# Remainder rows in one load per input, an earlier release of loads, and a scaled identity made by ScalarE

## The chip, the cores and the metric

One of the cores of one Trainium2 chip runs the whole program. The metric is device time in microseconds of that core, from one launch to its end; the kernel before took 313.18 us (median of 3 runs). The five engines of the core have queues of their own: PE (TensorE), DVE (VectorE), ACT (ScalarE), POOL (GpSimd) and SP (SyncE). POOL issues all loads here, SP all stores.

## The reference: what is computed

Four batches of q, k and v come as float32 arrays of 6336 rows by 256 channels. Attention works across channels, then a gated feed-forward layer follows, row by row:

```python
qn = q / (norm(q, axis=1) + 1e-06);  kn = k / (norm(k, axis=1) + 1e-06)
s = kn.transpose(0, 2, 1) @ qn / tau            # 256 x 256 per batch
a = softmax(s, axis=-1)
x = (v @ a).reshape(25344, 256)
H = maximum(x @ w_h, 0);  T = sigmoid(x @ w_t + b_t)
out = T * H + (1 - T) * x
```

## The kernel before, in words

**Tiles.** A tile is 128 rows of one input by 256 channels. The 6336 rows of a batch are 49 full tiles and 64 rows over, the remainder. A load casts float32 to 16-bit float on the way; it brings 4 to 17 tiles, and the remainder of each batch comes by a small load of its own (lines 109 to 125): qr and kr into tiles of their own, that of v into the last slot of the batch's third v load. Loads are numbered through: five of q and five of k a batch (q0 to q19, k0 to k19, a ring of six buffers each), three of v a batch (v0 to v11, a ring of four).

**Phase 1** (`p1_tile`) runs over the 50 tiles of a batch and sums on PE the product S of k and q (line 185) and, in G, the products of k and of q with themselves (lines 188 and 191), whose diagonals are the squared norms.

**The chain** (`chain`, ten steps) turns S and G of a batch into the matrices `mr` of phase 2. Its steps: the diagonals on DVE (`junk`, line 209), the root by a power on POOL (`nrm`, line 216), the reciprocal on DVE (`inv`, line 222), the identity scaled by `inv` and 1/tau (`dcat`, line 225, two instructions on DVE), a PE product with a matrix of ones that spreads this row of factors over all partitions (`cq`, line 233), logits on DVE, exponentials on ACT (`ar`, with a table load before and one behind), the softmax scale on ACT, a transpose and two products with the weights on PE.

**Phase 2** takes 25 steps a batch, 100 in all, each for a pair of tiles of v. In step t (line 523) PE computes the gate sums z into one of two banks that hold the bias already (`zbank`), transposes the pair of step t + 3 (`vtps`, line 340), then computes h and x; all three are line 363. ACT takes the sigmoid (`tt`, line 393), copies the transposed pair for even t (`vts`, line 355; DVE does it for odd t; the last pair of a batch, with 64 rows in its second tile, is copied in two pieces, line 353) and refills the bank with the bias (line 397). DVE forms `th` and `ux` (lines 405 and 410), POOL subtracts them into the output tile (`o`, line 416), and SP stores each four steps (line 388). `vtps` has one buffer; h, x, `cq` and other chain products share three; `th` and `ux` have five each.

**The order of the work** is written out by hand. The first batch's phase 1 runs alone, then its chain, then the 100 steps; in between the steps PE takes tiles of the next batch's phase 1, by the table KNOTS (all 150 are done at step 64). The chains of batches 1, 2 and 3 begin at steps 19, 44 and 64, and their steps are spread over the following ones by STEPS. A chain step stands ahead of ("pre"), behind ("post") or behind the PE part ("pe") of a step's own work, on every engine on which it issues.

**The release of loads** is planned when the program is built. `want` (line 431) lists the loads by the step that needs them; after each step `next_loads` (line 462) puts up to two of them into POOL's queue, if their ring buffer is free by then and if, in a small model of the DMA queue (0.315 us a tile, stores counted in), the load that stands eight places back has landed. In the running kernel POOL stands at a load until the one eight places back has landed.

Of the kernel before, what the change touches and what calls it, by code (L numbers as in the profile page):

```python
# [9 lines left out]
AluOp = mybir.AluOpType  # L10
Act = mybir.ActivationFunctionType
# [8 lines left out]
def kernel(  # L20
# [73 lines left out]

    q_t, k_t, qr_t, kr_t, v_t = {}, {}, {}, {}, {}

# [16 lines left out]
    def load_kr(b):  # L113
        kr_t[b] = stream_pool.tile([P, C], f16, tag="k_rem", bufs=2, name=f"kr{b}")
        nc.gpsimd.dma_start(out=kr_t[b][0:REM, :], in_=k[b][NF:N, :])

    def load_v(m):
        b, g = VALL[m]
        s0, ns = VG[b][g]
        v_t[m] = stream_pool.tile([P, 18, C], f16, tag="v_in", bufs=VRING, name=f"v{m}")  # L120
        nc.gpsimd.dma_start(out=v_t[m][:, 0:ns, :], in_=rows(v[b])[:, s0 : s0 + ns, :])

    def load_vr(b):
        g = len(VG[b]) - 1
        nc.gpsimd.dma_start(out=v_t[VFIRST[b] + g][0:REM, VG[b][g][1], :], in_=v[b][NF:N, :])

# [10 lines left out]
    ones32 = const_pool.tile([P, P], f32, tag="ones32")  # L137
    nc.vector.memset(ones32, 1.0)
    half = const_pool.tile([P, 4], f32, tag="half")
    nc.vector.memset(half, 0.5)  # L140
# [18 lines left out]
    load_k(NQG)  # L159
    load_v(0)  # L160

    def hx_tile(name):
# [6 lines left out]
    def p1_tile(b, j):  # L169
# [4 lines left out]
        if j == NS:  # L174
            kk, qq, nr = kr_t[b], qr_t[b], REM
# [24 lines left out]
    def chain(b):  # L200
# [19 lines left out]
        def invs():  # L220
            inv = work_pool.tile([P, 4], f32, tag="inv", name=f"inv{b}")
            nc.vector.reciprocal(out=inv, in_=st["nrm"])
            dcat = work_pool.tile([P, 2, P], f32, tag="dcat", bufs=1, name=f"dcat{b}")
            for c in range(2):
                nc.vector.tensor_scalar(
                    out=dcat[:, c, :], in0=ident0, scalar1=inv[:, 2 + c : 3 + c],
                    scalar2=inv_tau, op0=AluOp.mult, op1=AluOp.mult,
                )
            st.update(inv=inv, dcat=dcat)

        def pe_cq():
            cq = hx_tile(f"cq{b}")
            nc.tensor.matmul(cq[:, 0, :], ones32, st["dcat"][:, :, :], start=True, stop=True)
            st["cq"] = cq
# [86 lines left out]

    vT_t = {}
    o_t = {}
    NSLOT = B * NPAIR

    def v_of(b, s):
        g = max(i for i in range(len(VG[b])) if VG[b][i][0] <= s)
        return v_t[VFIRST[b] + g], s - VG[b][g][0]

# [3 lines left out]
    def transpose(t):  # L333
        b, i = divmod(t, NPAIR)
        vt, s = v_of(b, 2 * i)
        ps = psum_pool.tile([P, 2, 2, P], f32, tag="vT", name=f"vtps{t}")
        nr = nrows(i)
        for u in range(2):
            for c in range(2):
                nc.tensor.matmul(  # L340
                    ps[:, u, c, 0 : nr[u]], vt[0 : nr[u], s + u, bass.ts(c, P)],
                    ident[0 : nr[u], 0 : nr[u]],
                    start=(u == 0 and c == 0), stop=(u == 1 and c == 1),
                )
        return ps

    def vt_copy(t, ps):
        i = t % NPAIR
        sb = work_pool.tile([P, 2, 2, P], f16, tag="vTs", bufs=LOOK + 2, name=f"vts{t}")
        cp = nc.vector.tensor_copy if t % 2 else nc.scalar.copy  # L350
        if i == NPAIR - 1:
            for u, r in enumerate(nrows(i)):
                cp(out=sb[:, u, :, 0:r], in_=ps[:, u, :, 0:r])
        else:
            cp(out=sb, in_=ps)  # L355
        vT_t[t] = sb
# [75 lines left out]
    for n in range(NQG + 1, B * NQG):  # L432
# [4 lines left out]
        want.append((at, len(want), load_k, n, dep, QG[b][g][1]))  # L437
    for b in range(1, B):
        at = p1_slot((b - 1) * (NS + 1) + NS)
        want.append((at - 1, len(want), load_qr, b, None, 0.5))  # L440
        want.append((at - 1, len(want), load_kr, b, None, 0.5))
    for m in range(1, len(VALL)):
# [3 lines left out]
        want.append((at, len(want), load_v, m, dep, VG[b][g][1]))  # L446
        if g == len(VG[b]) - 1:
            want.append((at, len(want), load_vr, b, None, 0.5))
    want.sort()
# [3 lines left out]
    LANES = 8  # L453
    TILE_US = 0.315
    landing = [0.0] * LANES
# [134 lines left out]
```

## Time and profile before

| | |
|---|---|
| median of 3 runs (lowest to highest) | 313.18 us (312.12 to 313.43) |
| the profiled execution | 313.83 us, its span 312.1 us |
| PE busy in the span | 267.4 us (86%) |
| DVE, ACT, POOL busy | 172.6, 162.8, 170.7 us |
| DMA moved | 65.58 MB, mean 210 GB/s |
| HBM read, written | 78.38 MB, 25.95 MB |
| granted TensorE clock, mean | 0.954 |

Rows of the profile name the engine, the line of the kernel, the operation and the tiles (written <- read). In a row of idle time, "<-" names what ended the wait. Times in rows of the timeline are from the start of the span; the span leaves out 1.76 us of the profiled execution's own time.

### The profile page before, as it was taken

The numbers are of one execution on the slowest core, as the hardware profiler recorded it, in microseconds if no ns is written. First come the engines' busy times: TensorE is split into PE (matmuls) and PEld (weight loads), VectorE is DVE, ScalarE is ACT, GpSimd is POOL, SyncE is SP. The second block draws the span as 40 slices with busy tenths as digits, with TensorE's granted clock in tenths as the row PEclk, the third lists the DMA queues.
The fourth block names the chain that finished last, engine by engine and source line by source line (L and its number), as shares of the span: only waits on it lengthen the run. The fifth ranks groups of instructions, "written<-read, shape, count | busy, mean of one in ns | idle before, by whom it ended". The sixth has DMA issues, their size and how long they took to land.

```text
span 312.1 us, 6905 instructions
## 1 busy us (share of the span) xinstructions
PE 267.4 (86%) x2844; PEld 233.2 (75%) x2844; DVE 172.6 (55%) x321; ACT 162.8 (52%) x298; POOL 170.7 (55%) x184
## 2 busy tenths in 40 slices
PE   0498977999999899999999429999999868999990
PEld 0397854999999687999997318798998645999960
DVE  0000023775555746666668503555557947999990
ACT  1000055654455586565567613455556677898860
POOL 6112330865555755665667502755557644788881
PEclk9999967999999999999999957999999979999996
DMA  6999999999989999999968596999999951435434
GB/s 119 213 215 214 211 209 219 215 253 285 232 222 211 246 263 235 264 266 250 307 110 222 152 209 108 244 236 247 243 269 260 202 214 41 162 135 221 186 137 160
DMA packets 13377, 65.58 MB, mean 210 GB/s; under 512 B 1569, under 2 KB 3618, under 8 KB 8738
## 3 DMA queue, kind: packets, MB, share of 16 engines
q0 software_dynamic: 8992, 39.19, 64.5%
q1 hardware_dynamic: 4354, 25.96, 20.7%
q8 instruction: 22, 0.36, 0.4%
q14 instruction: 9, 0.07, 0.1%
HBM read 78.38 MB, written 25.95 MB: 334 GB/s over the span
## 4 chain that ended last, share of the span: by engine, by line
PE 62%; DMA 17%; DVE 6%; POOL 5%; ACT 4%; issue 3%; POOLq 0%; DVEq 0%
PE h L363 11%; PE zbank L363 11%; PE x L363 11%; PE S L185 10%; DMA k<-in_k_dram 9%; DMA v<-in_v_dram 8%; PE vtps L340 6%; PE G L191 5%; PE G L188 5%; POOL o L416 2%; DVE ux L410 2%; DVE th L405 2%; DVE junk L209 1%; POOL k L107 1%; PE ah L286 1%
## 5 line engine op out<-in xcount | busy, mean ns | idle before, releaser
L416 POOL TENSOR_TENSOR o<-th,ux 128x512 f32<-128x512 f32 x96 | 124.2, 1295 | 104.4 <-DVE ux L410 81.3
L363 PEld LDWEIGHTS <-vts 128*128 128x128 f16 x1200 | 111.1, 99 | 17.3 <-issue 5.0
L185 PE MATMUL S<-q,k 128*128 128x256 f16 x392 | 90.2, 284 | 13.7 <-DMA k<-in_k_dram 13.6
L393 ACT ACTIVATE tt<-zbank 128x512 f32<-128x512 f32 x100 | 59.7, 597 | 79.3 <-PE zbank L363 78.7
L405 DVE SCALAR_TENSOR_TENSOR th<-h,tt 128x512 f32<-128x512 f32 (+1 forms) x104 | 68.8, 665 | 56.7 <-PE h L363 40.8
L188 PE MATMUL G<-k 128*128 128x128 f16 x392 | 78.8, 226 | 0.0
L410 DVE SCALAR_TENSOR_TENSOR ux<-tt,x 128x512 f32<-128x512 f32 (+1 forms) x104 | 67.8, 655 | 0.8 <-PE x L363 0.7
L363 PE MATMUL x<-mr,vts 128*128 128x256 f16 (+1 forms) x400 | 61.9, 277 | 0.9 <-DVE th L405 0.9
L363 PE MATMUL h<-mr,vts 128*128 128x256 f16 (+1 forms) x400 | 61.9, 277 | 0.0
L363 PE MATMUL zbank<-mr,vts 128*128 128x256 f16 (+1 forms) x400 | 61.6, 276 | 0.0
L397 ACT COPY zbank<-btb 128x512 f32<-128x512 f32 x98 | 58.7, 599 | 1.6
L191 PE MATMUL G<-q 128*128 128x128 f16 x392 | 55.8, 226 | 0.0
L185 PEld LDWEIGHTS <-k 128*128 128x128 f16 x392 | 39.9, 102 | 18.0 <-DMA k<-in_k_dram 14.0
L340 PE MATMUL vtps<-ident,v 128*128 128x128 f16 (+1 forms) x400 | 40.0, 223 | 14.0 <-DMA v<-in_v_dram 10.0
L355 DVE CAST vts<-vtps 128x512 f16<-128x512 f32 x48 | 33.0, 687 | 25.8 <-PE vtps L340 25.8
L340 PEld LDWEIGHTS <-v 128*128 128x128 f16 (+1 forms) x400 | 30.9, 100 | 18.7 <-DMA v<-in_v_dram 10.5
L188 PEld LDWEIGHTS <-k 128*128 128x128 f16 x392 | 39.9, 102 | 1.2 <-issue 0.3
L191 PEld LDWEIGHTS <-q 128*128 128x128 f16 x392 | 31.6, 102 | 2.9
L355 ACT CAST vts<-vtps 128x512 f16<-128x512 f32 x48 | 27.9, 580 | 9.9 <-PE vtps L340 9.8
L209 DVE SCALAR_TENSOR_TENSOR junk<-G,ident 128x128 f32<-128x128 f32 x16 | 3.7, 287 | 36.5 <-PE G L191 36.5
L488 ACT COPY btb<-btp 128x256 f32<-128x256 f32 x2 | 0.6, 375 | 37.5 <-PE btp L485 37.5
L101 POOL DMA_DIRECT2D q<-in_q_dram x20 | 11.3, 567 | 6.6 <-DMA q<-in_q_dram 4.5
(55 smaller groups left out, 102.8 us busy)
## 6 DMA issues: line engine op xcount, KB each, us to landing
out_dram<-o SPq DMA_DIRECT2D x24, 1024.0 KB, 7.7
q<-in_q_dram POOLq DMA_DIRECT2D x12, 768.0 KB, 18.2
k<-in_k_dram POOLq DMA_DIRECT2D x12, 768.0 KB, 18.2
v<-in_v_dram POOLq DMA_DIRECT2D x8, 1024.0 KB, 9.8
v<-in_v_dram POOLq DMA_DIRECT2D x4, 1088.0 KB, 18.0
q<-in_q_dram POOLq DMA_DIRECT2D x4, 576.0 KB, 8.5
k<-in_k_dram POOLq DMA_DIRECT2D x4, 576.0 KB, 12.0
q<-in_q_dram POOLq DMA_DIRECT2D x4, 256.0 KB, 9.7
```

Of the source, the lines that this page charges most:

```text
L101: nc.gpsimd.dma_start(out=q_t[n][:, 0:ns, :], in_=rows(q[b])[:, s0 : s0 + ns, :])
L185: nc.tensor.matmul(S[:, c, :], kc, qq[0:nr, :], start=first and c == 0, stop=last and c == 1)
L188: nc.tensor.matmul(G[:, c, :], kc, kc, start=first and c == 0, stop=False)
L191: nc.tensor.matmul(G[:, 2 + c, :], qc, qc, start=False, stop=last and c == 1)
L340: nc.tensor.matmul(ps[:, u, c, 0 : nr[u]], vt[0 : nr[u], s + u, bass.ts(c, P)], ident[0 : nr[u], 0 : nr[u]], start=(u == 0 and c == 0), st ...
L355: cp(out=sb, in_=ps)
L363: nc.tensor.matmul(dst[0:r, u, :], sb[:, u, kt, 0:r], mr[:, kt, off : off + C], start=(not seeded and kt == 0 and (u == 0 or i == NPAIR - 1)),
L393: nc.scalar.activation(out=tt, in_=z, func=Act.Sigmoid)
L397: nc.scalar.copy(out=z, in_=btb)
L405: nc.vector.scalar_tensor_tensor(out=th[pr, us, :], in0=h[pr, us, :], scalar=0.0, in1=tt[pr, us, :], op0=AluOp.max, op1=AluOp.mult,)
L410: nc.vector.scalar_tensor_tensor(out=ux[pr, us, :], in0=tt[pr, us, :], scalar=1.0, in1=x[pr, us, :], op0=AluOp.subtract, op1=AluOp.mult,)
L416: nc.gpsimd.tensor_tensor(out=ot[pr, o0 + us.start : o0 + us.stop, :], in0=th[pr, us, :], in1=ux[pr, us, :], op=AluOp.subtract,)
```

## The change

Three things are changed.

The remainder rows of all four batches come in one load per input, 64 rows by 4 x 256 channels, into tiles that stay for the whole kernel. Those of q and k stand where the small loads of the first batch stood; that of v stands behind v0, where no load stood. The nine small loads of batches 1 to 3 and the first batch's small load of v are gone from the plan.

The model of the queue counts 0.305 us a tile, and a load is let out when the load eight places back lands, by the model, within the next 4 us.

The scaled identity is made by two ACT copies with the reciprocal as scale, and 1/tau stands in the matrix that multiplies it on PE (`taus`). Three copies of transposed pairs (vts24, vts50, vts72) go from ACT to DVE.

```diff
-    def load_qr(b):
-        qr_t[b] = stream_pool.tile([P, C], f16, tag="q_rem", bufs=2, name=f"qr{b}")
-        nc.gpsimd.dma_start(out=qr_t[b][0:REM, :], in_=q[b][NF:N, :])
...
+    def load_rem(name, src):
+        rem_t[name] = const_pool.tile([P, B, C], f16, tag=f"rem_{name}", name=f"rem_{name}")
+        nc.gpsimd.dma_start(
+            out=rem_t[name][0:REM, :, :], in_=src[:, NF:N, :].rearrange("b p c -> p b c")
+        )
...
-    load_qr(0)
-    load_kr(0)
+    load_rem("q", q)
+    load_rem("k", k)
...
     load_v(0)
+    load_rem("v", v)
...
             for c in range(2):
-                nc.vector.tensor_scalar(
-                    out=dcat[:, c, :], in0=ident0, scalar1=inv[:, 2 + c : 3 + c],
-                    scalar2=inv_tau, op0=AluOp.mult, op1=AluOp.mult,
+                nc.scalar.activation(
+                    out=dcat[:, c, :], in_=ident0, func=Act.Copy,
+                    scale=inv[:, 2 + c : 3 + c],
                 )
...
-            nc.tensor.matmul(cq[:, 0, :], ones32, st["dcat"][:, :, :], start=True, stop=True)
+            nc.tensor.matmul(cq[:, 0, :], taus, st["dcat"][:, :, :], start=True, stop=True)
...
+    on_dve = {t + LOOK for e, o in zip((19, 44, 64), STEPS[1:]) for t in (e + o[4], e + o[4] + 1)}
...
-        cp = nc.vector.tensor_copy if t % 2 else nc.scalar.copy
+        cp = nc.vector.tensor_copy if t % 2 or t in on_dve else nc.scalar.copy
...
-    TILE_US = 0.315
+    TILE_US = 0.305
+    SLACK = 4.0
...
-            if landing[-LANES] > now:
+            if landing[-LANES] > now + SLACK:
                 return
...
-    for tiles in (1, 1, 4, 4, 16):
+    for tiles in (1, 1, 4, 4, 16, 2):
         note_load(tiles, 0.0)
-    next_loads(3, landing[-LANES])
+    next_loads(2, landing[-LANES])
```

How instructions move is seen in the order of each engine's queue. First POOL before, from the adds of steps 42 and 43 through the norms of chain 2 to v6 (names as in the text, with a running buffer number behind):

```order
L416 TENSOR_TENSOR o41_2415<-th42_2455,ux42_2456 128x512
L416 TENSOR_TENSOR o41_2415<-th43_2496,ux43_2497 128x512
L216 TENSOR_TENSOR nrm2_2521<-n2_2_2514,half_84 128x4
L217 TENSOR_TENSOR nrm2_2521<-nrm2_2521,eps_86 128x4
L416 TENSOR_TENSOR o41_2415<-th44_2548,ux44_2549 128x512
L416 TENSOR_TENSOR o45_2589<-th45_2585,ux45_2586 128x512
L416 TENSOR_TENSOR o45_2589<-th46_2618,ux46_2619 128x512
L121 DMA v6_2627<-in_v_dram 128x4096
L101 DMA q17_2629<-in_q_dram 128x3072
```

Now POOL in the changed kernel, around the add of step 33, and at the norms of chain 2:

```order
L419 TENSOR_TENSOR o29_1909<-th32_2033,ux32_2034 128x512
L419 TENSOR_TENSOR o33_2079<-th33_2075,ux33_2076 128x512
L113 DMA v6_2081<-in_v_dram 128x4096
L419 TENSOR_TENSOR o33_2079<-th34_2119,ux34_2120 128x512
L419 TENSOR_TENSOR o33_2079<-th35_2160,ux35_2161 128x512
L101 DMA q17_2165<-in_q_dram 128x3072
...
L419 TENSOR_TENSOR o41_2417<-th42_2459,ux42_2460 128x512
L113 DMA v7_2464<-in_v_dram 128x4096
L419 TENSOR_TENSOR o41_2417<-th43_2502,ux43_2503 128x512
L101 DMA q19_2507<-in_q_dram 128x3072
L216 TENSOR_TENSOR nrm2_2529<-n2_2_2522,half_86 128x4
```

v6 went from behind the add of step 46 to behind that of step 33, and the power of chain 2 (`nrm2`) now has the load q19 between it and the add of step 43. The same place of chain 1 on POOL, before:

```order
L121 DMA v3_1321<-in_v_dram 128x4096
L416 TENSOR_TENSOR o16_1272<-th18_1365,ux18_1366 128x512
L101 DMA q12_1370<-in_q_dram 128x3072
L107 DMA k12_1372<-in_k_dram 128x3072
L216 TENSOR_TENSOR nrm1_1406<-n2_1_1399,half_84 128x4
```

and in the changed kernel:

```order
L107 DMA k13_1330<-in_k_dram 128x3072
L419 TENSOR_TENSOR o16_1279<-th18_1374,ux18_1375 128x512
L101 DMA q14_1379<-in_q_dram 128x3072
L216 TENSOR_TENSOR nrm1_1413<-n2_1_1406,half_86 128x4
L217 TENSOR_TENSOR nrm1_1413<-nrm1_1413,eps_88 128x4
```

One load stands between the add of step 18 and the power, where two stood. Last ACT at chain 1, before (`tt` is the sigmoid, `vts` the copy of a transposed pair, the copies from `btb` refill a bank):

```order
L393 ACTIVATE tt19_1428<-zbank1_435 128x512
L355 CAST vts22_1430<-vtps22_1413 128x512
L397 COPY zbank1_435<-btb_429 128x512
L393 ACTIVATE tt20_1469<-zbank0_432 128x512
L397 COPY zbank0_432<-btb_429 128x512
L393 ACTIVATE tt21_1503<-zbank1_435 128x512
L353 CAST vts24_1505<-vtps24_1488 128x256
L353 CAST vts24_1505<-vtps24_1488 128x2x64
```

and in the changed kernel:

```order
L396 ACTIVATE tt19_1435<-zbank1_437 128x512
L358 CAST vts22_1437<-vtps22_1420 128x512
L400 COPY zbank1_437<-btb_431 128x512
L225 ACTIVATE dcat1_1450<-ident0_75,inv1_1448 128x128 x2
L396 ACTIVATE tt20_1474<-zbank0_434 128x512
L400 COPY zbank0_434<-btb_431 128x512
L396 ACTIVATE tt21_1506<-zbank1_437 128x512
```

The two instructions of `dcat1` stand ahead of the sigmoid of step 20, and the two pieces of vts24 have left ACT's queue.

More of the change, by code (lines that the diff above doesn't have):

```diff
@@ L92, in rows @@
         return src2d[0:NF, :].rearrange("(p s) c -> p s c", s=NS)
-    q_t, k_t, qr_t, kr_t, v_t = {}, {}, {}, {}, {}
+    q_t, k_t, v_t = {}, {}, {}
     def load_q(n):
@@ L107, in load_k @@
         nc.gpsimd.dma_start(out=k_t[n][:, 0:ns, :], in_=rows(k[b])[:, s0 : s0 + ns, :])
-    def load_qr(b):
-        qr_t[b] = stream_pool.tile([P, C], f16, tag="q_rem", bufs=2, name=f"qr{b}")
-        nc.gpsimd.dma_start(out=qr_t[b][0:REM, :], in_=q[b][NF:N, :])
-    def load_kr(b):
-        kr_t[b] = stream_pool.tile([P, C], f16, tag="k_rem", bufs=2, name=f"kr{b}")
-        nc.gpsimd.dma_start(out=kr_t[b][0:REM, :], in_=k[b][NF:N, :])
     def load_v(m):
@@ L119, in load_v @@
         s0, ns = VG[b][g]
-        v_t[m] = stream_pool.tile([P, 18, C], f16, tag="v_in", bufs=VRING, name=f"v{m}")
+        v_t[m] = stream_pool.tile([P, 17, C], f16, tag="v_in", bufs=VRING, name=f"v{m}")
         nc.gpsimd.dma_start(out=v_t[m][:, 0:ns, :], in_=rows(v[b])[:, s0 : s0 + ns, :])
-    def load_vr(b):
-        g = len(VG[b]) - 1
-        nc.gpsimd.dma_start(out=v_t[VFIRST[b] + g][0:REM, VG[b][g][1], :], in_=v[b][NF:N, :])
+    rem_t = {}
+    def load_rem(name, src):
[3 more added lines that the diff above has]
+        )
     load_q(0)
@@ L138 @@
     nc.vector.memset(ones32, 1.0)
+    taus = const_pool.tile([P, P], f32, tag="taus")
+    nc.vector.memset(taus, inv_tau)
     half = const_pool.tile([P, 4], f32, tag="half")
@@ L174, in p1_tile @@
         if j == NS:
-            kk, qq, nr = kr_t[b], qr_t[b], REM
+            kk, qq, nr = rem_t["k"][:, b, :], rem_t["q"][:, b, :], REM
         else:
@@ L326, in v_of @@
     def v_of(b, s):
+        if s == NS:
+            return rem_t["v"][:, b, :]
         g = max(i for i in range(len(VG[b])) if VG[b][i][0] <= s)
-        return v_t[VFIRST[b] + g], s - VG[b][g][0]
+        return v_t[VFIRST[b] + g][:, s - VG[b][g][0], :]
     def nrows(i):
@@ L338, in transpose @@
         for u in range(2):
+            vt = v_of(b, 2 * i + u)
             for c in range(2):
                 nc.tensor.matmul(
-                    ps[:, u, c, 0 : nr[u]], vt[0 : nr[u], s + u, bass.ts(c, P)],
+                    ps[:, u, c, 0 : nr[u]], vt[0 : nr[u], bass.ts(c, P)],
                     ident[0 : nr[u], 0 : nr[u]],
@@ L437 @@
         want.append((at, len(want), load_k, n, dep, QG[b][g][1]))
[L438 to L441, printed above, removed]
     for m in range(1, len(VALL)):
```

3 lines of the change are left out of this document (removed).

## The prediction

> **What bounds the kernel now.** I read the page first, then the busy time by stretches of 5 us, then the timeline of each engine around the worst stretches, last the landing times of single loads. The page (slices of 7.8 us) shows TensorE's granted clock and the DMA engines, and the cost of the final add:
>
> ```profile
> PEclk9999967999999999999999957999999979999996
> DMA  6999999999989999999968596999999951435434
> L416 POOL TENSOR_TENSOR o<-th,ux 128x512 f32<-128x512 f32 x96 | 124.2, 1295 | 104.4 <-DVE ux L410 81.3
> ```
>
> The DMA engines are full from the start to slice 19, have holes in slices 20 to 24 (156 to 195 us) and are full again. The clock falls in slice 23. The stretches (time, length, then busy us of PE, PEld, DVE, ACT and POOL, clock, DMA share, GB/s):
>
> ```profile
> 90.00:95.00 5.00, 5.00 (x61) 4.64 (x60) 2.45 (x5) 2.52 (x5) 3.62 (x4) 1.00 0.70 121
> 170.00:175.00 5.00, 3.61 (x35) 2.83 (x33) 4.96 (x10) 2.93 (x6) 3.00 (x4) 1.00 0.49 192
> 175.00:180.00 5.00, 0.62 (x8) 0.32 (x5) 0.76 (x2) 4.02 (x7) 2.38 (x3) 1.00 0.42 69
> 180.00:185.00 5.00, 0.00 (x0) 0.00 (x0) 0.00 (x0) 0.00 (x0) 0.00 (x0) 0.60 1.03 214
> 185.00:190.00 5.00, 4.73 (x31) 3.86 (x32) 1.45 (x3) 1.98 (x4) 1.60 (x2) 0.50 0.54 111
> 190.00:195.00 5.00, 5.00 (x59) 4.58 (x57) 1.81 (x3) 1.77 (x3) 0.73 (x2) 0.88 0.86 153
> 210.00:215.00 5.00, 4.66 (x55) 4.06 (x53) 2.38 (x5) 2.65 (x5) 3.07 (x3) 1.00 1.05 213
> 265.00:270.00 5.00, 5.00 (x52) 4.38 (x52) 4.80 (x11) 3.80 (x8) 3.24 (x5) 1.00 0.65 251
> ```
>
> So the middle is paced by PE (5.00 of 5.00) except where PE waits; the end, from 265 us, by VectorE (4.80 of 5), and nothing in the change touches that stage. The worst wait is seen on PE: the first use of v6 (step 47 transposes for step 50), and the same place one batch earlier, v3 in step 22. The mains of step 25 (121.64) and of step 50 (199.36) end the two stages that I compare.
>
> ```profile
> 110.33 0.39 PE L340 MATMUL vtps<-ident,v 128*128 128x128 f16 x4
> 121.64 0.60 PE L363 MATMUL zbank<-mr,vts 128*128 128x256 f16 x4
> 185.27 0.61 PE L340 MATMUL vtps<-ident,v 128*128 128x128 f16 x4 [9.65 <-DMA v<-in_v_dram]
> 199.36 0.60 PE L363 MATMUL zbank<-mr,vts 128*128 128x256 f16 x4
> ```
>
> PE stood 9.65 us for v6. Why v6 was late: its issue on POOL. Below are the issues of k11, v5 and v6, and from the DMA view of those moments the landing time of each, in the same order.
>
> ```profile
> 92.28 0.54 POOL L107 DMA_DIRECT2D k<-in_k_dram  x1
> 125.64 0.57 POOL L121 DMA_DIRECT2D v<-in_v_dram  x1
> 177.06 0.61 POOL L121 DMA_DIRECT2D v<-in_v_dram  x1
> ```
> ```profile
> k<-in_k_dram POOLq DMA_DIRECT2D x1, 576.0 KB, 10.4
> v<-in_v_dram POOLq DMA_DIRECT2D x1, 1088.0 KB, 27.4
> v<-in_v_dram POOLq DMA_DIRECT2D x1, 1024.0 KB, 8.2
> ```
>
> v5 waited 27.4 us in a full queue; v6 landed 8.2 us after an issue that came when the queue was empty (DMA share 0.49 and 0.42). Nothing held POOL there: the instruction stands late in POOL's order.
>
> **Loads let out earlier.** In the new order v6 stands behind the add of step 33 instead of step 46, 13 steps sooner. A step takes (175.02 - 121.64) / 22 = 2.43 us, where 175.02 = 185.27 - 9.65 - 0.60 is the mains of step 47. So v6 is issued near 177.06 - 13 x 2.43 = 145.5. Its landing is then set by the queue. k11 landed at 92.28 + 10.4 = 102.7, v5 at 125.64 + 27.4 = 153.0; between them 121 tiles (v3 16, q12 and k12 24, v4 16, q13 to k14 48, v5 17), so 50.3 / 121 = 0.416 us per tile, stores included. Behind v5 come q15, k15, q16, k16, v6: 42 tiles, 17.5 us.
>
> The remainder loads change v5's own landing: three loads of 2 tiles come ahead of it (6 x 0.416 = 2.5 us), five small ones of 0.5 go (1.04), and the hole at 90 to 95 (DMA 0.70 against 1.05 when full: 5 x 0.35 / 1.05 = 1.7 us) closes because q11 is now let out behind step 6. v5 lands at 153.0 + 2.5 - 1.04 - 1.7 = 152.8 and v6 at 170.3, against 175.6 needed, less 1.2 gained in chain 1 (below): 4 us to spare. The same rate puts k17 (24 tiles on) at 180.3, k18 (24) at 190.3 and v7 (16) at 196.9. v7's wait of before, the 0.34 us missing in 210 to 215, was at 213.7; with the gain up to there, 9.65 + 2.78 + 1.5 in two chains, it is needed near 199.5. So both waits go, with 2.5 us to spare at the second. What is late next is v5: used at 153.5 before, about 152.3 now, it costs 0.5 us (0 to 1.2).
>
> Gain: 9.65 + 0.34. The stop has a second price. The clock is 0.60, 0.50 and 0.88 in the three stretches after it. From the first transposes to the mains three steps on takes 121.64 - 110.33 = 11.31 us in batch 1, and 199.36 - 185.27 = 14.09 in batch 2, with the same instructions: 2.78 us for the slow clock.
>
> The Trainium skill (TensorE: Matmul & The Clock Gate, What's actually happening) says that the gate goes back to full rate after one busy window of about 3.4 us; by that half a window, 1.7 us, would be lost and the sum would come out 1.1 us higher. The rows show the half clock for longer, so I take 2.78.
>
> **The first remainder loads.** rem_q and rem_k carry all four batches and stand behind k4, whose landing is 12.31 + 22.5 = 34.8. Four tiles at 0.416, too high for a stretch without stores, make 36.5.
>
> ```profile
> 12.31 0.54 POOL L107 DMA_DIRECT2D k<-in_k_dram  x1 [3.10 <-DMA k<-in_k_dram]
> k<-in_k_dram POOLq DMA_DIRECT2D x1, 256.0 KB, 22.5
> 38.22 0.28 PE L185 MATMUL S<-qr,kr 64*128 64x256 f16 x1
> ```
>
> Their first use is at 38.22, behind PE's work on k3 and k4: cost 0, with 1.7 us of cover.
>
> **Scaled identity on ACT.** PE's wait for it, in the view of waits, and the three chains that lie in full work (chain 1 with POOL's add and ACT's sigmoid of step 20; then chains 2 and 3):
>
> ```profile
> PE cq L233 <- DVE dcat L225: 6.1, 4, 2.0
> ```
> ```profile
> 104.77 0.60 ACT L393 ACTIVATE tt<-zbank 128x512 f32<-128x512 f32 x1
> 105.54 1.28 POOL L416 TENSOR_TENSOR o<-th,ux 128x512 f32<-128x512 f32 x1
> 105.62 0.18 DVE L222 RECIPROCAL inv<-nrm 128x4 f32<-128x4 f32 x1 [0.34 <-POOL nrm L217]
> 105.83 1.27 DVE L225 TENSOR_SCALAR dcat<-ident,inv 128x128 f32<-128x128 f32 x2
> 107.25 0.67 PE L233 MATMUL cq<-dcat,ones 128*128 128x256 f32 x2 [1.42 <-DVE dcat L225]
> ...
> 170.51 0.18 DVE L222 RECIPROCAL inv<-nrm 128x4 f32<-128x4 f32 x1
> 170.72 1.52 DVE L225 TENSOR_SCALAR dcat<-ident,inv 128x128 f32<-128x128 f32 x2
> 172.39 0.67 PE L233 MATMUL cq<-dcat,ones 128*128 128x256 f32 x2 [1.39 <-DVE dcat L225]
> ...
> 242.02 0.17 DVE L222 RECIPROCAL inv<-nrm 128x4 f32<-128x4 f32 x1
> 242.23 1.53 DVE L225 TENSOR_SCALAR dcat<-ident,inv 128x128 f32<-128x128 f32 x2
> 243.91 0.67 PE L233 MATMUL cq<-dcat,ones 128*128 128x256 f32 x2 [1.26 <-DVE dcat L225]
> ```
>
> The pair took 1.27 to 1.53 us while an add ran on POOL. For ACT the nearest row is its smallest copy, 128 columns in 273 ns (the lower of its two forms):
>
> ```profile
> L353 ACT CAST vts<-vtps x4: 273/322/367, 108.9 to 257.4; 128x256 f16<-128x256 f32 x2, 128x128 f16<-128x128 f32 x2
> ```
>
> Two make 0.55 us (0.73 by the upper end), and 0.15 on to PE as before. Chain 1: POOL's power step now stands behind one load instead of two, 0.54 sooner, so inv is there at 105.26, dcat at 105.8, when PE is just free (107.25 - 1.42 = 105.83); I take 1.2 of the 1.42. Chain 2: the power step now stands behind q19, 0.57 later, so inv is at 171.26 and cq at 171.96: 0.4, I take 0.3. Chain 3: 242.19 + 0.70 = 242.9, a gain of 1.0. Chain 0, idle engines: 0.06 lost. Sum 2.4. The new wait sits on ACT: dcat stands ahead of the next sigmoid, so ACT stands for inv up to 1 us, and the sigmoid (104.77 before), the copies of vts and the refill of the bank queue behind it; the VectorE product waits for that sigmoid, but it waited behind dcat before. Bounds: all PE waits gone, 4.1, to 1 us lost in each chain, -3.
>
> The Trainium skill (ScalarE: Activation LUTs, Rules for kernel authors and What ACT_TABLE_LOAD costs) speaks against this move: multiplications belong on VectorE, and an ACTIVATE with one pointer operand is given as 280 ns + 0.833 ns per column, an estimated 0.68 us for the pair with their overlap. By it the sum would be 0.4 us higher.
>
> **Copies moved to VectorE.** Of vts24, vts50 and vts72 only the last stands behind the exponentials with PE waiting:
>
> ```profile
> 252.10 0.58 ACT L355 CAST vts<-vtps 128x512 f16<-128x512 f32 x1
> 252.74 0.59 PE L340 MATMUL vtps<-ident,v 128*128 128x128 f16 x4 [2.73 <-ACT vts L355]
> ```
>
> PE may start long before, but the next product waits for the sigmoid ahead of it; I count ACT's 0.58 (0 to 1.4).
>
> **The sum.** The profiled execution took 313.83 us (span 312.1), 0.65 above the median of 313.18; 313.83 - 9.65 - 2.78 - 0.34 - 2.4 - 0.58 + 0.5 = 298.6.
>
> **Rivals.** *Another load takes the place.* The queue is now always full, so a late load is no longer a late issue but a slow rate. v5 and v7 have -0.5 and 2.5 us to spare. A wait of 4 us at either costs 4 + 2.8, with the clock: 305.5. For it: those margins; against: the rate is measured with stores in it.
>
> *The engines are the bound.* Bytes are unchanged. From k11 to v7 stand 227 tiles, 94.4 us; if the rate were 13% worse, all landings would be 12 us later and the stop would only move: 312.6. Against: shares of 0.49, 0.42 and 0.54 in three of the four stretches from 170 to 190 are room.
>
> *POOL stands at the loads.* The ninth load stands until the first has landed (the 3.10 us above k4's row), and a load may now be let out up to 4 us before that. POOL's adds and norms queue behind it, and through the buffers of th and ux VectorE and PE. Two steps have 2 x (2.43 - 1.295) - 0.55 = 1.72 us free per load; with 24 loads in the stage, a mean stand of 3 us makes 24 x 1.28 = 31 lost: 329. It decides from 1.72 us and is slower than before from 2.35. Against: k13, eight loads ahead of v6, lands at 152.8 - 41 x 0.416 = 135.7, and v6 is issued at 145.5.
>
> **How the numbers follow.** Both waits gone: 0.75. Another load: 0.13. Engines: 0.05. POOL: 0.07. The range goes from 295.5 (4.1 and 1.4 us for the last two terms, no wait for v5) to 305.5, the first rival. A run can tell about 0.5% (1.6 us) from no change: faster 0.88, same 0.05, slower 0.07.
>
> **What would show it.** Right: no wait on v over 1 us, clock 1.00 from 55 to 240, DMA share near 1 from 55 to 210, v6 issued near 145, cq waits near 0.2, 1.0 and 0.2, span near 297. Wrong: a new DMA wait on PE, POOL standing for loads in mid-kernel, or ACT's sigmoid starting over 2 us later than PE's bank is ready in the chains.

## The result and the profile after

The changed kernel takes 296.93 us (median of 4 runs, 296.72 to 297.11), beside 312.65 us (310.42 to 313.43, 4 runs) for the kernel before on the same chip. The ratio is 0.951, with an interval from 0.946 to 0.956. The profiled execution took 296.72 us, its span 294.7, its mean granted clock was 0.983.

On the page, the clock and the DMA rows (slices now of 7.4 us) answer to those of before:

```profile
span 294.7 us, 6910 instructions
PEclk9999988999999999999999999999999979999997
DMA  6999999999999999999999999999996631245434
```

The holes of the DMA engines in mid-kernel are closed up to slice 29, and the dip of the clock at slice 23 is gone. One dip is left, in slice 32. The busy times by stretches show both places (columns as before):

```profile
175.00:180.00 5.00, 4.83 (x62) 4.30 (x61) 2.51 (x5) 4.12 (x8) 2.56 (x4) 1.00 1.05 290
180.00:185.00 5.00, 5.00 (x49) 3.18 (x47) 2.83 (x7) 2.71 (x6) 3.23 (x4) 1.00 1.06 218
185.00:190.00 5.00, 5.00 (x62) 4.64 (x60) 3.17 (x5) 2.75 (x5) 1.67 (x2) 1.00 1.01 280
...
235.00:240.00 5.00, 3.22 (x18) 2.22 (x18) 3.15 (x6) 3.42 (x7) 2.10 (x2) 0.70 0.14 54
```

Where PE did nothing before, it is now busy for 4.83 to 5.00 of 5 us at full clock. POOL issues v5, v6 and v7 at the times below; how long each then takes to land (last column, us) is in the DMA view of those moments, in the same order:

```profile
114.56 0.58 POOL L113 DMA_DIRECT2D v<-in_v_dram  x1
...
142.73 0.58 POOL L113 DMA_DIRECT2D v<-in_v_dram  x1
...
164.47 0.58 POOL L113 DMA_DIRECT2D v<-in_v_dram  x1
```
```profile
v<-in_v_dram POOLq DMA_DIRECT2D x1, 1088.0 KB, 35.1
v<-in_v_dram POOLq DMA_DIRECT2D x1, 1024.0 KB, 25.0
v<-in_v_dram POOLq DMA_DIRECT2D x1, 1024.0 KB, 28.7
```

They land at 149.7, 167.7 and 193.2. PE uses them first at 151.18, 172.85 and 198.29, so they are there 1.5, 5.2 and 5.1 us ahead, and PE waits for none of them. In the chains the scaled identity now comes from ACT (the three product rows are those of chains 1, 2 and 3; the last row groups all eight instructions, with lowest, mean and highest ns):

```profile
104.27 0.17 DVE L222 RECIPROCAL inv<-nrm 128x4 f32<-128x4 f32 x1
104.47 0.69 ACT L225 ACTIVATE dcat<-ident,inv 128x128 f32<-128x128 f32 x2 [0.60 <-DVE inv L222]
105.22 0.70 PE L233 MATMUL cq<-dcat,taus 128*128 128x256 f32 x2 [0.32 <-ACT dcat L225]
...
169.75 0.70 PE L233 MATMUL cq<-dcat,taus 128*128 128x256 f32 x2 [1.06 <-ACT dcat L225]
...
227.55 0.70 PE L233 MATMUL cq<-dcat,taus 128*128 128x256 f32 x2 [0.32 <-ACT dcat L225]
```
```profile
L225 ACT ACTIVATE dcat<-ident,inv x8: 384/394/403, 41.7 to 227.1; 128x128 f32<-128x128 f32 x8
```

PE's wait for `cq` fell from 1.42, 1.39 and 1.26 us to 0.32, 1.06 and 0.32. To say where the span went I compare when PE reaches the same instruction in both traces, each of one profiled execution. The first use of q6 and the gate sums of step 99 frame the stretch in which the change works; before:

```profile
56.01 0.27 PE L185 MATMUL S<-q,k 128*128 128x256 f16 x1
...
301.73 0.72 PE L363 MATMUL zbank<-mr,vts 128*128 128x256 f16 x4
```

and after:

```profile
54.98 0.27 PE L185 MATMUL S<-q,k 128*128 128x256 f16 x1
...
285.09 0.72 PE L366 MATMUL zbank<-mr,vts 128*128 128x256 f16 x4
```

Between these marks 245.7 us became 230.1. Marks in between split it as follows:

| place | predicted | measured |
|---|---|---|
| start to q6 (chain 0 in it) | +0.06 | -1.03 |
| chain 1 | -1.2 | -1.28 |
| v5 late | +0.5 | 0 |
| chain 2 | -0.3 | -0.30 |
| the stop at v6 | -9.65 | -9.81 |
| slow clock behind it | -2.78 | -2.49 |
| the wait for v7 | -0.34 | -0.50 |
| chain 3 | -1.0 | -0.91 |
| chain 3 to step 99 (vts72) | -0.58 | -0.31 |
| step 99 to the end of the span | 0 | -0.72 |
| sum | -15.3 | -17.4 |

### The profile page after: what moved, and what is told of

The parts are those of the page before. It is cut to its first block, busy times and chain, and to the rows that moved or that the text cites. A ratio compares the mean times of both kernels' runs of the same rounds, so it can differ in the third digit from the quotient of the medians.

```text
span 294.7 us, 6910 instructions
## 1 busy us (share of the span) xinstructions
PE 262.0 (89%) x2844; PEld 228.7 (78%) x2844; DVE 169.5 (58%) x318; ACT 163.5 (55%) x302; POOL 166.4 (56%) x175
## 4 chain that ended last, share of the span: by engine, by line
PE 72%; DMA 9%; ACT 6%; POOL 5%; DVE 4%; issue 2%; POOLq 0%; DVEq 0%
PE zbank L366 13%; PE x L366 13%; PE h L366 13%; PE S L185 11%; DMA k<-in_k_dram 9%; PE vtps L343 7%; PE G L188 6%; PE G L191 6%; POOL o L419 2%; DVE th L408 1%; PE ah L286 1%; DVE ux L413 1%; ACT tt L396 1%; ACT dcat L225 1%; PE cq L233 1%
## 5 line engine op out<-in xcount | busy, mean ns | idle before, releaser
L366 PEld LDWEIGHTS <-vts 128*128 128x128 f16 x1200 | 109.7, 98 | 19.3 <-issue 7.9
L185 PE MATMUL S<-q,k 128*128 128x256 f16 x392 | 88.0, 278 | 14.3 <-DMA k<-in_k_dram 14.3
L188 PE MATMUL G<-k 128*128 128x128 f16 x392 | 77.0, 223 | 0.0
L366 PE MATMUL h<-mr,vts 128*128 128x256 f16 (+1 forms) x400 | 61.0, 274 | 0.0
L185 PEld LDWEIGHTS <-k 128*128 128x128 f16 x392 | 39.0, 100 | 18.6 <-DMA k<-in_k_dram 15.0
L358 DVE CAST vts<-vtps 128x512 f16<-128x512 f32 x50 | 34.3, 687 | 20.3 <-PE vtps L343 20.3
L188 PEld LDWEIGHTS <-k 128*128 128x128 f16 x392 | 39.1, 100 | 1.1 <-issue 0.3
L343 PE MATMUL vtps<-ident,v 128*128 128x128 f16 x392 | 38.4, 220 | 1.6 <-DVE vts L358 1.2
L343 PEld LDWEIGHTS <-v 128*128 128x128 f16 x392 | 30.0, 98 | 5.2 <-issue 2.8
L358 ACT CAST vts<-vtps 128x512 f16<-128x512 f32 x46 | 26.7, 580 | 2.3 <-PE vtps L343 2.3
L107 POOL DMA_DIRECT2D k<-in_k_dram x20 | 11.3, 566 | 5.6 <-DMA k<-in_k_dram 5.3
```

The costliest lines, as they stand in the source:

```text
L107: nc.gpsimd.dma_start(out=k_t[n][:, 0:ns, :], in_=rows(k[b])[:, s0 : s0 + ns, :])
L185: nc.tensor.matmul(S[:, c, :], kc, qq[0:nr, :], start=first and c == 0, stop=last and c == 1)
L188: nc.tensor.matmul(G[:, c, :], kc, kc, start=first and c == 0, stop=False)
L343: nc.tensor.matmul(ps[:, u, c, 0 : nr[u]], vt[0 : nr[u], bass.ts(c, P)], ident[0 : nr[u], 0 : nr[u]], start=(u == 0 and c == 0), stop=(u = ...
L366: nc.tensor.matmul(dst[0:r, u, :], sb[:, u, kt, 0:r], mr[:, kt, off : off + C], start=(not seeded and kt == 0 and (u == 0 or i == NPAIR - 1)),
```

## The experiments

The theory was that the loads' part removes the stop and what hangs on it (some 12.8 us), and that the identity and the copies bring some 3 more. The rivals were that only one of the loads' two edits works, that a gain in the chains is eaten by a load that comes no sooner, and that POOL pays for loads let out early. The kernels ran on four chips, on which the kernel before took 312.32 to 312.48 us (medians). Runs of one kernel lie up to 3.8 us apart (the kernel before; 3.7 in e3). Part of this goes with the clock they were granted: e4 below took 301.89 at a mean clock of 0.961 and 300.37 at 0.982. Not all does: the slowest run of e11, 299.00, had a higher clock (0.981) than its fastest, 297.51 (0.973). Kernels that lie within 1 us are therefore compared between the two marks, not by time alone. The marks come from one execution of each kernel, but a stretch that an edit doesn't touch repeats closely: steps 25 to 44 take 46.11 to 46.12 us in 13 of the 14 traces (46.75 in e3).

**e1: the release alone**, on the kernel before.

```diff
-    TILE_US = 0.315
+    TILE_US = 0.305
+    SLACK = 4.0
-            if landing[-LANES] > now:
+            if landing[-LANES] > now + SLACK:
```

> The kernel before with the earlier release alone (0.305 us a tile, loads let out up to 4 us ahead of the model); remainder loads and the scaled identity as before. In POOL's order v6 stands behind the add of step 39 (before: 46, changed kernel: 33), so it is issued near 177.06 - 7 x 2.43 = 160 and lands near 168, ahead of the 175.6 at which PE needs it. Theory (the stop for v6 is its late place in POOL's order, and any place early enough removes it whole): the stop of 9.65 us, the 2.5 us of slow clock behind it and the 0.5 us at v7 go, 312.65 - 12.65 = 300.0 us (299 to 301), PE's longest wait for v under 1 us. Rival (both parts are needed, since the small loads still stand in the queue): v6 stays late by about half, 305 us or more, and a wait for v of 4 us or more is left.

Measured: 301.67 us (ratio 0.964, 0.958 to 0.970). v6 goes out at 158.63, and the two worst stretches are full:

```profile
158.63 0.58 POOL L121 DMA_DIRECT2D v<-in_v_dram  x1
```
```profile
175.00:180.00 5.00, 5.00 (x65) 4.68 (x63) 1.66 (x4) 4.96 (x9) 1.85 (x2) 1.00 1.01 298
180.00:185.00 5.00, 4.94 (x49) 3.21 (x47) 3.18 (x8) 4.14 (x9) 3.10 (x3) 1.00 1.05 232
```

The time is a little above the theory's range (the runs go from 300.25 to 302.59, at clocks from 0.982 to 0.970), and far from the rival. The release alone removes the whole stop.

**e2: the merged remainder loads alone**: the changed kernel with the old model, identity and copies.

```diff
-    TILE_US = 0.305
-    SLACK = 4.0
+    TILE_US = 0.315
+    SLACK = 0.0
-                nc.scalar.activation(
-                    out=dcat[:, c, :], in_=ident0, func=Act.Copy,
-                    scale=inv[:, 2 + c : 3 + c],
+                nc.vector.tensor_scalar(
+                    out=dcat[:, c, :], in0=ident0, scalar1=inv[:, 2 + c : 3 + c],
+                    scalar2=inv_tau, op0=AluOp.mult, op1=AluOp.mult,
...
-    on_dve = {t + LOOK for e, o in zip((19, 44, 64), STEPS[1:]) for t in (e + o[4], e + o[4] + 1)}
+    on_dve = set()
```

> The changed kernel with the merged remainder loads alone: model at 0.315 us a tile, no time ahead, scaled identity and copies on VectorE as before. v6 stands behind the add of step 37, issued near 155. Theory (place in the order is all): the same 300.0 us (299 to 301), no wait for v over 1 us. Rival (the gain comes from the time ahead, merging saves only bytes of small packets): 308 us or more with a wait for v of 4 us or more.

Measured: 299.81 us (0.958, 0.954 to 0.963). v6 goes out sooner still:

```profile
154.90 0.57 POOL L113 DMA_DIRECT2D v<-in_v_dram  x1
```

So either edit on the loads is enough by itself. Together, without the small parts, they take 301.66 us (e4), 1.9 us more than the merged loads alone, and no run of e4 is as fast as the slowest of e2: on top of the merged loads the earlier release is a loss here. Merged loads with the identity on ACT but without the earlier release were not run, so whether the changed kernel needs that release stays open. The rival fell.

**e3: the scaled identity on ACT alone**, on the kernel before (the same lines as in the change, with `taus`).

> The kernel before with the scaled identity on ScalarE alone; loads as before, so v6 still stands behind the add of step 46. Theory (the pair on VectorE stands while POOL's add runs, and ScalarE does not): the pair takes about 0.5 us in every chain, chains 1, 2 and 3 gain 1.4, 0.3 and 0.9 us, and since v6's issue stands behind PE's own work it comes earlier with it: 312.65 - 2.6 = 310.0 us. Rival (what chains 1 and 2 gain is lost again in the stop for v6, which ends when it ends): only chain 3's 0.9 is left, 311.7 us, and the stop grows by 1.7 to 11.3 us.

Measured: 312.14 us (10 runs, 0.999, 0.996 to 1.002), no difference. The rival's time was right, its place only in part. The first uses of v6 and of v7 in this trace, that of the slowest of the ten runs (314.28):

```profile
184.35 0.61 PE L342 MATMUL vtps<-ident,v 128*128 128x128 f16 x4 [10.08 <-DMA v<-in_v_dram]
...
213.48 0.40 PE L342 MATMUL vtps<-ident,v 128*128 128x128 f16 x4 [2.57 <-DMA v<-in_v_dram]
```

The stop at v6 grew from 9.65 to 10.08 and the one at v7 from 0.34 to 2.57. PE comes sooner and waits longer: the gain in the chains is given back to loads that don't come sooner.

**e4: both edits on the loads, without identity and copies**: the changed kernel with the second and third part of e2's diff.

> The changed kernel with the scaled identity and the three copies back on VectorE; both changes to the loads stay. Theory: the chains lose 2.6 us (1.4, 0.3, 0.9), the copies 0.3: 296.93 + 2.9 = 299.8 us, the pair takes 1.2 to 1.5 us again where an add of POOL runs. Rival (with the loads in time the chains are hidden beside other work): within 0.5 us of 296.93.

Measured: 301.66 us (0.964, 0.959 to 0.968). Neither expectation is exact: against the changed kernel 4.7 us are missing, 3.9 of them between the marks (chain 1 1.1, chain 2 1.7, the stretch of v6 0.25, chain 3 0.85). So the identity, worth nothing alone (e3), is worth something once the stop is gone. How much is less sure than the 3.9 looks: some 1.25 of it is a slow clock behind chain 2 (below) that e2, which lacks the small parts as well, doesn't have; e2 is 2.3 us longer between the marks than the changed kernel. Chain 2 shows more than I counted:

```profile
171.09 1.30 POOL L419 TENSOR_TENSOR o<-th,ux 128x512 f32<-128x512 f32 x1
171.38 1.28 DVE L225 TENSOR_SCALAR dcat<-ident,inv 128x128 f32<-128x128 f32 x2
172.81 0.67 PE L233 MATMUL cq<-dcat,ones 128*128 128x256 f32 x2 [1.75 <-DVE dcat L225]
```

Behind q19 the norms come later, and the pair on DVE runs into POOL's add on top of that: PE waits 1.75 us here, 1.06 in the changed kernel. A second price of 1.0 us follows it up to step 47, and some 0.25 behind it, in the clock of the next stretches:

```profile
174.00:176.00 2.00, 2.00 (x14) 1.49 (x14) 1.81 (x5) 1.95 (x3) 1.24 (x1) 0.59 1.03 230
176.00:178.00 2.00, 2.00 (x17) 1.66 (x15) 0.56 (x1) 1.97 (x6) 1.36 (x2) 0.56 1.04 308
```

In the changed kernel the clock stays at 1.00 at this place. The length of the wait alone does not decide it: in e1 PE waits 2.27 us for `cq` in chain 2, and the clock stays at 1.00.

**e5: the three copies back on ACT**: the changed kernel with `on_dve = set()`.

> The changed kernel with the three copies of transposed pairs (vts24, vts50, vts72) back on ScalarE. Theory (the scaled identity carries nearly all of the 4.7 us that the two edits are worth together, 301.66 against 296.93): the copies are worth 0.6 us, 297.5 us (297.0 to 298.2). Rival (the three copies carry the part that the waits for the scaled identity, 2.6 us, leave open): 299.0 us or more.

Measured: 298.47 us (0.956, 0.953 to 0.959), 1.5 above the changed kernel, but between the marks only 0.22 us longer. In the profiled execution, the slowest of the four (299.26), the rest lies ahead of q6, in a stretch that the edit doesn't touch. At chain 3, the copy's row in e5 and the one row of a wait that stands there in the changed kernel:

```profile
238.84 0.38 PE L343 MATMUL vtps<-ident,v 128*128 128x128 f16 x4 [2.80 <-ACT vts L358]
```
```profile
236.78 0.79 PE L366 MATMUL x<-mr,vts 128*128 128x256 f16 x4 [2.19 <-DVE th L408]
```

With the copy on DVE, PE no longer waits for it and then waits for `th` of that step, which needs the sigmoid behind the same exponentials on ACT. The stop only changes its name; this is the dip of slice 32. The dip itself costs nothing: e10 below has a stop of 2.18 us at this place without it, and takes the same 57.0 us from step 67 to step 99.

**e6: v6 kept back** (and all behind it) until the step that let it out before.

```diff
+            if fn is load_v and arg == 6 and step[0] < 46:
+                return
```

> The changed kernel with one rule more: v6, and what stands behind it in the plan, is not let out before step 46, where it stood in the kernel before; all else as in the changed kernel. Theory (the stop is made by the place in the order): v6 is issued near 175 behind the add of step 46, lands 8 us later, PE stands about 10 us for it from 173, the clock falls and costs 2.5 us more, v7 is late by 0.3 to 3 us: 296.93 + 14 = 311 us (309 to 313). Rival (the stop was a matter of the bytes in the queue, and merged remainders and closed holes have removed it): under 300 us.

Measured: 309.71 us (2 runs, 0.992, 0.990 to 0.995).

```profile
175.40 0.61 POOL L113 DMA_DIRECT2D v<-in_v_dram  x1
183.60 0.61 PE L343 MATMUL vtps<-ident,v 128*128 128x128 f16 x4 [10.30 <-DMA v<-in_v_dram]
```
```profile
177.15:187.39 10.24, 3.79 (x24) 3.05 (x25) 2.15 (x4) 0.99 (x3) 0.66 (x1) 0.50 0.83 170
```

The stop is back with 10.30 us, and so is the half clock, from 177.15 to 187.39. The kernel loses 12.8 us against the changed one, 12.0 of them between the marks: 10.5 at the stop, 1.45 to the slow clock from there to step 50, 0.75 at v7, less 0.7 in chains 1 and 2. The place of one load in POOL's order carries most of the result.

**e7: loads let out up to 12 us ahead** (SLACK 4 to 12).

> The changed kernel with loads let out 12 us ahead of the model instead of 4; v6 behind the add of step 29, others about 4 steps sooner as well. Theory (POOL comes to a load long after the one eight places back has landed, about 10 us at v6): POOL stands for loads under 1 us each and the time stays, 296.9 us (296.2 to 297.6). Rival of the prediction (POOL stands at the loads): a mean stand of over 1.72 us at some 24 loads, 298.5 us or more.

Measured: 303.69 us (0.972, 0.970 to 0.975). The theory fell. All of the loss between the marks, 6.5 us, arises in chain 1:

```profile
107.22 0.57 POOL L113 DMA_DIRECT2D v<-in_v_dram  x1 [2.81 <-DMA v<-in_v_dram]
107.81 1.04 POOL L216 TENSOR_TENSOR nrm<-n,half 128x4 f32<-128x4 f32 x1
109.38 0.69 ACT L225 ACTIVATE dcat<-ident,inv 128x128 f32<-128x128 f32 x2 [5.01 <-DVE inv L222]
110.12 1.22 PE L233 MATMUL cq<-dcat,taus 128*128 128x256 f32 x2 [4.73 <-ACT dcat L225]
```

POOL stands 2.81 us at v5 for the landing of an earlier load, the power of the norms waits behind it, and through `inv` and `dcat` PE stands 4.73 us (0.32 in the changed kernel). The clock adds to it: it is at half from 108.47 to 115.30 us. The rival's bound of 298.5 held, its place did not: what hurts here is not many small stands of POOL but one in front of a chain.

**e8: loads let out up to 30 us ahead.**

> The changed kernel with loads let out 30 us ahead of the model; v6 behind the add of step 24, nine steps or 22 us sooner, more than the 10 us of margin. POOL must now stand at loads. By the price of the prediction's rival (every microsecond over 1.72 at each of 24 loads is lost): POOL stands over 50 us in all and the time is 303 us or more. Other theory (the adds may lag five steps, the buffers of th and ux take the stands up): 299 us or less with the same stands.

Measured: 302.43 us (0.969, 0.967 to 0.971), between the two. The stands of POOL at loads, in the view of waits (total, count, longest):

```profile
POOL v L113 <- DMA k<-in_k_dram: 12.6, 3, 5.2
POOL k L107 <- DMA k<-in_k_dram: 11.4, 4, 3.3
POOL k L107 <- DMA q<-in_q_dram: 7.8, 3, 3.5
POOL v L113 <- DMA v<-in_v_dram: 5.0, 2, 2.6
```

They make 36.8 us. Of the second row 5.3 us belong to the start and stand in the changed kernel too; with smaller rows that are not shown, POOL stands 36 us at 14 loads from 45 us on, and at none in the changed kernel. Yet the kernel loses only 5.5 against it. Between the marks 4.9 us are lost in chain 1 and 1.5 ahead of it, and 0.6 are won in chain 2. The 1.5 us show what else a stand can do:

```profile
89.37 0.57 POOL L113 DMA_DIRECT2D v<-in_v_dram  x1 [3.65 <-DMA k<-in_k_dram]
91.29 0.69 DVE L408 SCALAR_TENSOR_TENSOR th<-h,tt 128x512 f32<-128x512 f32 x1 [3.28 <-POOL o L419]
92.03 0.60 PE L366 MATMUL x<-mr,vts 128*128 128x256 f16 x4 [1.45 <-DVE th L408]
```

POOL's adds come late behind the load, DVE waits 3.28 us for one of them before it can write the next `th`, and PE waits 1.45 us for DVE. Five buffers each of `th` and `ux` lie between POOL and the engines that feed it, and here they are used up. The other stands cost PE no wait ahead of chain 1.

**e9: the identity on DVE, in the form that also sums** (the row sum is written out in addition, and nothing reads it).

```diff
+            dsum = work_pool.tile([P, 2], f32, tag="dsum", name=f"dsum{b}")
...
-                nc.scalar.activation(
-                    out=dcat[:, c, :], in_=ident0, func=Act.Copy,
-                    scale=inv[:, 2 + c : 3 + c],
+                nc.vector.tensor_scalar(
+                    out=dcat[:, c, :], in0=ident0, scalar1=inv[:, 2 + c : 3 + c],
+                    scalar2=inv_tau, op0=AluOp.mult, op1=AluOp.mult,
+                    accum_out=dsum[:, c : c + 1],
...
-            nc.tensor.matmul(cq[:, 0, :], taus, st["dcat"][:, :, :], start=True, stop=True)
+            nc.tensor.matmul(cq[:, 0, :], ones32, st["dcat"][:, :, :], start=True, stop=True)
```

> The changed kernel with the scaled identity back on VectorE, but in the form that also writes a sum of each row (a sum that nothing reads; what the instruction makes of its second scalar may differ); the three copies stay on VectorE. Theory (in the plain form VectorE's instruction stands until POOL's add has ended, the form with a sum doesn't): the pair takes under 0.8 us in chains 1 to 3 though an add of POOL runs beside it, PE waits for it 0.3, 1.0 and 0.4 us, 297 us (296.3 to 298.5). Rival (any VectorE instruction on these operands stands while POOL adds): the pair takes 1.2 to 1.5 us, 300 us or more.

Measured: 297.21 us (0.950, 0.947 to 0.953), the same as the changed kernel. In chain 1:

```profile
105.09 1.27 POOL L421 TENSOR_TENSOR o<-th,ux 128x512 f32<-128x512 f32 x1 [0.30 <-DVE inv L222]
105.14 0.34 DVE L226 TENSOR_SCALAR_CACHE_REDUCE dcat<-ident,inv 128x128 f32<-128x128 f32 x1
...
105.90 0.67 PE L235 MATMUL cq<-dcat,ones 128*128 128x256 f32 x2 [0.34 <-DVE dcat L226]
```

The add runs on POOL until 106.36; the product of the finished pair starts on PE at 105.90. In e4 the pair took 1.28 us, to 172.66, while the add ran from 171.09 to 172.39: the plain form ends only behind the add, the form with a sum doesn't mind it. The Trainium skill (SBUF — State Buffer, Who interferes with whom) states such a rule: a VectorE `tensor_scalar` may take the port pair that it shares with GpSimd and then waits for the other's whole instruction, except in the form that writes its accumulator; the rows agree. The gain of this part of the change is therefore to be out of the way of POOL's add, not that ACT is the faster engine.

**e10: the norms ahead of the loads**: no load is let out in the step just ahead of each chain.

```diff
-        next_loads(2, now)
+        if t not in (18, 43, 63):
+            next_loads(2, now)
```

> The changed kernel without a load in POOL's queue between the last add ahead of a chain and the chain's power step (no load is let out at steps 18, 43 and 63; it comes one step later). Theory (a load of 0.58 us ahead of the power is on PE's path in chains 2 and 3, where PE waits 1.06 and 0.32 us for the product of the scaled identity): chain 1 no gain (POOL waits for the norms there), chain 2 0.55, chain 3 0.3: 296.0 us (295.3 to 296.8). Rival (ScalarE, blocked ahead of its sigmoid, sets the time): 296.9.

Measured: 297.12 us (0.951, 0.948 to 0.953); time can't tell it from the changed kernel. Between the marks it gains 0.7 us (229.4 for 230.1), 0.6 of it in chain 2:

```profile
170.08 0.70 PE L233 MATMUL cq<-dcat,taus 128*128 128x256 f32 x2 [0.47 <-ACT dcat L225]
```

The wait there falls from 1.06 to 0.47 with q19 out of the way; 1.0 us is lost again ahead of q6, where nothing was changed.

**e11: 12 us ahead, with the norms ahead of the loads** (e7 and e10 together).

> The kernel with loads let out 12 us ahead (303.69 us) with the same rule, so that no load stands between the add of step 18 and the power step of chain 1. Theory (of its 6.8 us nearly all is PE's 4.73 us for the scaled identity of chain 1, because POOL stood at v5 ahead of the power; adds that come late cost nothing): PE's wait for it falls under 2 us and the time to 299.5 us (298 to 301). Rival (the late adds cost it, through the buffers of th and ux): 302.5 us or more.

Measured: 297.61 us (0.953, 0.950 to 0.956).

```profile
104.17 1.04 POOL L216 TENSOR_TENSOR nrm<-n,half 128x4 f32<-128x4 f32 x1
106.49 0.70 PE L233 MATMUL cq<-dcat,taus 128*128 128x256 f32 x2 [0.74 <-ACT dcat L225]
```

The power starts as soon as the adds are done, 3.6 us sooner than in e7, and of e7's loss of 6.8 us 6.1 are gone. This settles e7: its loss was the load in front of the norms, with the slow clock behind it. POOL still stands 25 us at 13 loads from 45 us on in this trace, more than the 19 us of e7, so stands elsewhere cost little: between the marks it takes 229.85 us, beside 229.42 in e10.

**e12: e9 and e10 together** (1/tau stays in `taus`; the row sum is again one that nothing reads).

> The changed kernel with both mends that the profiles point to: the scaled identity on VectorE in the form that also writes a sum (0.61 us for the pair, and no wait of ScalarE ahead of its sigmoid), and no load ahead of the power step. Theory (between the first and the last mark of phase 2 the two are worth 0.6 to 1.0 us against the changed kernel, as the norms alone gave 0.69): the way from the first use of q6 to the mains of step 99 takes 229.4 to 229.8 us (before 245.72, changed kernel 230.11), 296.3 us (295.5 to 297.3). Rival (PE's waits moved there are taken up later): 230.1 us or more, 296.9 us or more.

Measured: 296.07 us (6 runs, 295.80 to 296.98; 0.948, 0.945 to 0.951). Between the marks it takes 229.35 us, a hair below what was expected, and 0.07 below e10. PE's wait for `cq` in chain 2 is 0.48 us. Its median is 0.86 us (0.3%) below the changed kernel's, and their runs overlap by 0.3 us: better by the marks, and hardly by time.

## Why the prediction was right

**The stop, and the clock behind it.** The step held: v6 was late only because its issue stood late. e6 moves that issue back and gets the stop again. The size held as well, 9.81 for 9.65. For the clock 2.49 was measured for 2.78, but that this price fits is in part the luck of the trace it was read from. Two more traces have the stop, e3 and e6. Their stretches at half clock, with that of the kernel before (e6's row stands above):

```profile
180.97:191.21 10.24, 5.94 (x39) 4.88 (x40) 1.45 (x3) 1.98 (x4) 2.34 (x3) 0.50 0.74 146
```
```profile
176.86:187.10 10.24, 2.75 (x17) 2.14 (x17) 1.09 (x2) 2.06 (x4) 0.63 (x2) 0.50 0.93 178
```

The half clock lasts 10.24 us in all three, but 5.94 us of PE's work fall into it before, 2.75 in e3 and 3.79 in e6. From the first transposes of v6 to the mains of step 50 the three take 14.09, 12.55 and 13.05 us, the changed kernel 11.60: the slow clock cost 2.49, 0.95 and 1.45 us for stops of nearly one length. The 1.7 us worked out from the Trainium skill's one busy window (TensorE: Matmul & The Clock Gate, What's actually happening) lie inside that range. So the prediction took for a fixed price of the stop what depends on where the half clock lies against it. What it did not see either is that each edit on the loads would have been enough by itself (e1, e2).

**The landings.** v6 was issued at 142.73 (predicted 145.5) and landed at 167.7 (170.3), v7 at 193.2 (196.9). From v5 on the rate held: from v5 to v6 18.0 us for 17.5, from v6 to v7 25.5 for 26.6. The step that failed is the sum for v5's landing: 149.7 for 152.8. Hence v5 costs nothing in place of 0.5. The three terms for the remainder loads and the hole all lie ahead of k11. k11 landed at 101.3, where they give 102.4; the 121 tiles from there to v5 then took 48.4 us, not 50.3 (0.400 us a tile, not 0.416). So 1.1 us of the miss lie in those terms and 2.0 in the rate of that stretch, carried over from the trace before. The program's earlier start has no part in it that shows: e4 and e5 reach q6 later than the kernel before (56.24 and 57.12 for 56.01), and v5 lands at 149.0 and 148.6 there. The remainder of k landed at 36.7, a shade past its bound of 36.5 and ahead of its use: no cost.

**The scaled identity.** The three chains gave 1.28, 0.30 and 0.91 us for 1.2, 0.3 and 1.0. The pair on ACT took 0.69 us, not 0.55: the 273 ns of a plain copy were the wrong row for an instruction with a scale pointer, which took 394. The Trainium skill's 280 ns + 0.833 ns a column (ScalarE: Activation LUTs, What ACT_TABLE_LOAD costs), an estimated 387 ns here, agrees. The three waits that are left make 1.70 us, 0.3 more than expected; chain 1 gave 0.2 us that do not lie in that wait, and the sum came out even. ACT's new wait for `inv` came to 0.60, 1.69 and 0.60 us (up to 1 was expected). In chain 2 the sigmoid starts 2.01 us behind its gate sums, just at what the prediction named as a sign of being wrong, but it costs nothing visible: in e9, where it starts at once, steps 44 to 47 take 6.94 us for 6.97. That the term belongs to the change as a whole, and is nought while the stop is there (e3), the prediction did not say.

**The copies.** This step failed: 0.58 us were counted for vts72. Some 0.31 appears behind chain 3, but e5, with the copy on ACT, shows 0.30 there as well, and e2 and e4 0.37, and so does e3 with 0.30, where the loads are as before and only the identity has moved. Only e1 shows nothing. So it is not the copy. In the two traces without this gain, that of the kernel before and e1, a stretch of 3.4 us at half clock begins just ahead of the end of PE's wait behind chain 3 (at 252.65 for a wait that ends at 252.74, and at 239.38 for 239.91); in the others it comes later or not at all. That would fit a price of the clock, and is argued, not shown. The next product waits for the sigmoid anyway, as the prediction said and then did not price.

**The rest.** The priced terms without v5 make 15.75 us; they measured 15.60. The forecast of 298.6 was 1.7 us high, for the start (1.1), the end of the span (0.7) and v5 (0.5), with some small terms the other way. In medians the kernel gained 15.7 us, nearer to the forecast's 15.25 than the 17.1 between the two profiled executions. The 1.03 us ahead of q6 go with a granted clock that differs between executions: from 45 to 55 us it was 0.91 and 1.00 here, 0.72 and 0.66 before, and over the twelve experiments this mark lies anywhere from 1.20 us earlier to 1.11 later, whatever was edited. The two traces with 3.4 us at half clock between 28 and 56 us reach q6 at 54.81 and 54.98, the eight with 6.8 us at 55.07 to 56.01, the four with 10.2 us at 56.01 to 57.12. No run sets the clock, so the cause is argued. The 0.7 us at the end lie behind the issue of the last store. All eleven kernels with the merged loads have them, and the three without (before, e1, e3) don't; why stays open.

**The rivals.** No other load took the place, and the queue's rate did not bound the kernel. POOL does not stand in mid-kernel with 4 us of slack; with 12 and 30 it does (e7, e8, e11), but the price that the prediction gave for it, so much for every load, was wrong: stands are absorbed, except in front of the norms (e7) and where the buffers of `th` run out (e8).

## What to carry to other kernels

When a transfer is late, look at where its issue stands in the queue of the engine that issues it before you look at bandwidth; if the queue was empty when it went out, its place in the order is the whole cause. A gain ahead of a stop for data is given back at that stop, so try small edits again once the stop is gone. Where loads and a short latency chain share one engine's queue, let loads out early, but not directly in front of that chain, and not so early that the stands use up the buffers behind them.

## What was not expected of the hardware

A plain `tensor_scalar` of 128 columns on DVE, with POOL's add running, makes the pair last 1.27 to 1.53 us; the form that also writes a sum takes 0.34 us each beside the same add (e9). The clock fell to half after a wait of 1.75 us on PE in e4 and not after one of 2.27 us in e1. In all fourteen traces its stretches at half rate between 20 and 285 us last 3.41, 6.83 or 10.24 us, and the same stop of some 10 us cost from 0.95 to 2.49 us by where such a stretch lay. And POOL stood 25 us for loads in mid-kernel in e11, which takes 297.61 us, while in e7 a load in front of the norms, with a stand of 2.81 us, put the power 3.6 us later and PE stood 4.73 us.
